# Reordering the TensorE products of the 63 steps that begin with a transform unit, in a fused spectral-mixing and hard-swish kernel

## The chip, the cores and the metric

The kernel runs on one core of one Trainium2 chip. The metric is the device time of one execution in microseconds; a kernel's time is the median of its runs. Beside it stands one profiled execution, whose trace gives the start and duration of each instruction on each engine: TensorE (PE, with its weight loads listed apart as PEld), VectorE (DVE), ScalarE (ACT), GpSimd (POOL) and SyncE (SP, which issues transfers here).

## What is computed

The reference is a global filter in the frequency domain, followed by a two-layer feed-forward block with hard-swish:

```python
X = np.fft.rfft(x, axis=1)                    # x: (8, 3008, 256)
Y = X * (filt_r + 1j * filt_i)[None]
y = np.fft.irfft(Y, n=3008, axis=1)
h = y.reshape(24064, 256) @ w_in              # w_in: (256, 2048)
g = h * np.clip(h + 3.0, 0.0, 6.0) / 6.0
out = g @ w_out                               # w_out: (2048, 256)
```

## The kernel before, in words

**Blocks and steps.** The 24064 tokens are cut into 47 blocks of 512, and the 2048 hidden columns into 8 parts of 256. One part of one block is a step, so there are 376 of them, in the order block by block and part by part. The first block (8 steps) is computed plainly. In the other 368 steps both matrix products are done as two-by-two block products with seven multiplications in place of eight. In step `i` the program issues the *up* products of its own part and, among them, the *down* (output) products of the part before, whose hidden values are then ready. The loop at the end of the function writes the order of a step out by hand, and each engine executes its own instructions in that order.

**The up products.** They are, in order of need, A11, S1, A12, S2, S4, S3 and A22 (in code `product(...)`, which ends in `strips` at L972). Each is 256 columns wide and is issued as two strips of 64 weight columns, four matmul records in all. They accumulate in two PSUM tiles with one buffer each: `al` takes A11, then S2, S3 and A22 on top of it; `be` takes S1 and S4 in one half and A12 in the other. Between them other engines read the partial sums:

- after A11, ACT copies `al` (L987, here called s0); after S1 and A12, ACT copies half of `be` (L988, s5); after S2, ACT copies `al` again (L997, s1);
- after S4, DVE adds `be` and the copies into the first hidden half (L1002, h0);
- after S3, DVE adds `al` and s5 into half of the second (L1007, h1);
- after A22, ACT copies `al` into the other half of the second (L1016, the h copy).

So S2 must wait for s0, S4 for s5, S3 for s1, A22 for h1, and whatever writes `al` next must wait for the h copy. The rectifier runs on ACT (L1021), once for each half, and the product with the hidden value on DVE (L1026).

**The output products.** DVE makes the seven operands from the hidden values: `g_sums` (L1026 for the second half, L1033, L1034) and `g_last` (L1039, which product 3 alone needs). The products are numbered 1 to 7. Each has two halves `u` of 128 columns; a half is four matmul records into a PSUM tile `po` that is read only at the end of a block. `down(k, p, *prods, us=...)` issues the numbered products in the order given.

**The transform units.** The transforms of the next batches are woven into these steps. `plan` says which function runs in which step and at which place of it. Three kinds of unit open a step (places 3 and 4 of the plan): the first stage (`a8_unit`, L608, 24 steps), the second stage (`b8_unit`, L706, 18 steps) and the inverse stage (`bi8_unit`, L779, 21 steps). Each consists of 32-row matmuls into four PSUM tiles, two of which are `al` and `be`. ACT copies these two out (L612, L712, L783), first `al`, then `be`. The step's own A11 and S1 write these tiles next, and so wait for the two copies.

In a step with a unit, `units` is a non-empty list, `inverse` is therefore true, and `ahead` is `(1, 2)`. No two such steps stand side by side; the step after one is always an ordinary step, which begins with A11. Product 3 of the step before can be held back behind the unit (`held`). Some steps also have an ACT copy for the next block's inputs (`t_copy`, L953) between the first rectifier and the h copy.

Of the kernel before, what the change touches and what calls it, by code (L numbers as in the profile page):

```python
# [53 lines left out]
NP = DFF // 256  # L54
# [175 lines left out]
def kernel(  # L230
# [602 lines left out]
    def pair(i):  # L833
        b, js, o, n = chunks[i]
        return b * HC * NA + o, n
# [134 lines left out]
    def strips(ps, w, x, **kw):  # L970
        for o in range(0, P, STRIP):
            nc.tensor.matmul(ps[ds(o, STRIP)], w[:, ds(o, STRIP)], x, skip_group_check=True, **kw)  # L972

    def product(ps, p, w, x, start=False, stop=False):
        strips(ps, w_in[p][:, w, :], x, start=start, stop=stop)
# [12 lines left out]
        nc.scalar.activation(out=s5, in_=be[:, 1, :], func=AXT.Copy)  # L988
        st["up"] = al, be, s, s5

    def up_2(k, p):
        t = st["xt", k]
        al, be, s, s5 = st["up"]
        h = [hp.tile([P, 512], FP32, name="h%d" % i) for i in range(2)]
        product(al, p, S2, t[:, F3, :])
        product(be[:, 1, :], p, S4, t[:, F5, :], stop=True)
        nc.scalar.activation(out=s[:, 1, :], in_=al, func=AXT.Copy)  # L997
        st["h"] = h
# [30 lines left out]
    def g_sums(k, p):  # L1029
        hswish(k, p, 1)  # L1030
        g = st["g", k, p]
        v = nc.vector
        v.tensor_tensor(out=g[:, G1, :], in0=g[:, G3, :], in1=g[:, G22, :], op=ALU.add)  # L1033
        v.tensor_tensor(out=g[:, G3:G2 + 1:2, :], in0=g[:, G3:G1 + 1, :],  # L1034
                        in1=g[:, G11:G11 + 1, :].broadcast_to([P, 2, 256]), op=ALU.subtract)

    def g_last(k, p):
        g = st["g", k, p]
        nc.vector.tensor_tensor(out=g[:, G4, :], in0=g[:, G12, :], in1=g[:, G2, :], op=ALU.subtract)  # L1039
# [7 lines left out]
    def down(k, p, *prods, us=(0, 1)):  # L1047
        g = st["g", k, p]
        if p == 0 and 1 in prods:
            st["po", k] = [psO.tile([P, 2, 2, P], FP32, name="po%d" % i) for i in range(4)]  # L1050
        for n in prods:
            bank, part = BANK[n]
            a, w = DOWN[n]
            for u in us:
                strips(st["po", k][bank][:, part, u, :], g[:, a, ts(u, P)], w_out[p][:, w, :],
                       start=(p == 0 and n in OPENS and u == 0), stop=(p == NP - 1 - (k == LAST)))

    def last_down():
        p, v, add = NP - 1, nc.vector.tensor_tensor, ALU.add
        g, o = st["g", LAST, p], st["o", LAST][0]  # L1060
        hswish(LAST, p, 1)
        ps = [psF.tile([P, 512], FP32, name="psf", tag="f") for t in range(2)]
        for i, a in ((0, G11), (1, G12)):
            for t in range(2):
                for u in range(2):
                    strips(ps[t][:, ts(u, D)], g[:, a + t, ts(u, P)], w_out[p][:, 2 * i:2 * i + 2, :].rearrange("p j m -> p (j m)"),
                           start=i == 0 and u == 0, stop=i == 1)
        out_4(LAST)
        v(out=o_at(LAST, 0, 1), in0=st["po", LAST][3][:, 1, :, :], in1=o_at(LAST, 0, 1), op=add)
        for t, qs in ((0, (nc.sync, nc.scalar)), (1, (nc.sync, nc.scalar))):  # L1070
            both = o[:, t, :, :].rearrange("p u d -> p (u d)")
            v(out=both, in0=ps[t], in1=both, op=add)
            store_last(t, qs)
# [6 lines left out]
    def plain_up(p):  # L1080
        st["g", 0, p] = gp.tile([P, 7, 256], FP32, name="g")
        st["h"] = [psU.tile([P, 512], FP32, name=n) for n in ("al", "be")]
        for i in range(2):
            for d in range(2):
                strips(st["h"][i], w_in[p][:, 2 * d + i, :], xn[:, d, :, 0:PAIRS], start=d == 0, stop=d == 1)
            relu(i)
            hswish(0, p, i)

    def plain_down(p, tokens=(0, 1)):
        g = st["g", 0, p]  # L1090
        if p == 0:
            st["po", 0] = [psO.tile([P, 2, 2, P], FP32, name="po%d" % i) for i in range(2)]
        for t in tokens:
            for u in range(2):
                for i, a in ((0, G11), (1, G12)):
                    strips(st["po", 0][t][:, u, :, :].rearrange("p a m -> p (a m)"), g[:, a + t, ts(u, P)],
                           w_out[p][:, 2 * i:2 * i + 2, :].rearrange("p j m -> p (j m)"),
                           start=p == 0 and u == 0 and i == 0, stop=p == NP - 1)
# [8 lines left out]
    def out_1(k):  # L1107
        po = st["po", k]
        p14 = p14p.tile([P, 2, 2, P], FP32, name="p14")
        nc.scalar.activation(out=p14, in_=po[0], func=AXT.Copy)  # L1110
        st["o", k] = op.tile([P, 2, 2, D], FP32, name="o", tag="o"), p14
# [76 lines left out]
    with tc.manual_schedule():  # L1188
# [120 lines left out]
        half = 0  # L1309
# [28 lines left out]
        for i in range(2, len(chunks)):  # L1338
            k = pair(i)[0] // PAIRS
# [57 lines left out]
        for n in range(1, B):  # L1397
            a_at, f_at, y_at, bi_at = places(n)
            if n > 1:
                k = (first[n] - 7) * NP  # L1400
# [4 lines left out]
            for c, s in enumerate(a_at):  # L1405
# [7 lines left out]
                k = (first[n] - 7) * NP  # L1413
# [44 lines left out]
        def late(i):  # L1458
            return i % NP in (1, 2) or any(fn in HEAVY for place in range(3) for fn, a in plan.get((i - 1, place), ()))

        held = None
        items = [(k, p) for k in range(NBLK) for p in range(NP)]
        for i in range(len(items) + 1):
            up = i < len(items)
            k, p = items[min(i, len(items) - 1)]
            dn = i > 0
            kd, pd = items[i - 1]
            def do(place):
                for fn, a in plan.get((i, place), ()):
                    fn(*a)  # L1470

            if k == 0:
                plain_up(p)
                do(0)
                if dn:
                    plain_down(pd)
                do(1)
                do(2)
                continue
            if not up:  # L1480
                last_down()
                break
            ends = k == LAST and p == NP - 1
            last_plain = dn and kd == 0
            dn = dn and kd > 0
            units = [fn for fn, a in plan.get((i, 3), ())]
            inverse = bool(units)
            ahead = (1, 2) if inverse else (1,) if units else ()
            if units:
                do(3)  # L1490
                if held:
                    down(*held, 3)
                g_sums(kd, pd)
                if not late(i):
                    g_last(kd, pd)
                do(4)
                down(kd, pd, *ahead)
                up_1(k, p)
                do(0)
                down(kd, pd, 4 if inverse else 2)  # L1500
            else:
                up_1(k, p)
                do(0)
                if dn:
                    g_sums(kd, pd)
                    if not late(i):
                        g_last(kd, pd)
                    down(kd, pd, 1)
            if up:
                up_2(k, p)  # L1510
            if dn and pd == 0 and kd > 1:
                out_4(kd - 1)
            if up:
                up_2b(k, p)
            if dn:
                down(kd, pd, *((5,) if inverse else (4,) if units else (2, 4)), us=(0,) if inverse else (0, 1))
                if pd == NP - 1:
                    out_1(kd)
            if up:
                up_3(k, p)  # L1520
                if dn and late(i) and not (pd == 0 and kd > 1):
                    g_last(kd, pd)
            if dn:
                down(kd, pd, 5, us=(1,) if inverse else (0, 1))
                down(kd, pd, 6)
            if up:
                up_4(k, p)
            if ends:
                out_1(k)
            if last_plain:  # L1530
                plain_down(pd, (0,))
            if dn and pd == 0 and kd > 1:
                out_5(kd - 1)
                g_last(kd, pd)
            if up:
                do(1)
                hswish(k, p, 0)
            if up:
                up_5(k, p)
            if last_plain:  # L1540
                plain_down(pd, (1,))
                plain_out()
            if dn:
                if pd == NP - 1 or ends:
                    out_2(kd)
                held = (kd, pd) if (i + 1, 3) in plan and any(fn is n_five for fn, a in plan.get((i, 0), ())) and kd not in kinds else None
                down(kd, pd, *((7,) if held else (7, 3)))
                if pd == NP - 1 or ends:
                    out_3(kd)
            do(2)  # L1550
# [30 lines left out]
```

## Time and profile before

| | |
|---|---|
| median of 3 runs | 2551.36 us (2550.79 to 2552.4) |
| the profiled execution | 2552.4 us, of which 2550.4 us is the span from first to last instruction |
| TensorE matmuls, busy | 2533.7 us (99%), 37890 records |
| TensorE weight loads, busy | 2000.0 us (78%) |
| VectorE, busy | 2016.9 us (79%) |
| ScalarE, busy | 1361.4 us (53%) |
| GpSimd, busy | 423.0 us (17%) |
| granted TensorE clock | 1.0 |
| transfers | 276.91 MB, mean 109 GB/s |

Busy time is the time in which at least one instruction of the engine was recorded as running. The ends of matmuls are modelled, so the 99% does not say that TensorE did useful work all the time; what it lost is seen in the distance from the start of one product to the start of the next. A record such as `MATMUL al<-xt,w_all ... x4` in the timeline is one whole up product; `po<-w_all,g x4`, `x8`, `x12` and `x16` are one to four halves of output products.

### The profile page before, as it was taken

What the parts mean: (1) busy time and instruction counts of PE and PEld (TensorE: products, weight loads), DVE (VectorE), ACT (ScalarE), POOL (GpSimd) and SP (SyncE); (2) the same over time, 40 slices, a digit from 0 to 9 for tenths busy, and PEclk for the clock granted to TensorE, in tenths of its full rate; (3) what the DMA queues carried; (4) which work ended last, traced back from release to release, by engine and by line L of the source; (5) the groups of instructions that cost most, each with busy time, mean ns of one, the idle gap of its engine ahead of it and who ended that gap; (6) DMA issues with size and microseconds to landing.
All of it is one profiled execution on the core that took longest, in us unless ns stands there. A gap on an engine that the chain in (4) does not pass through costs nothing.

```text
span 2550.4 us, 87284 instructions
## 1 busy us (share of the span) xinstructions
PE 2533.7 (99%) x37890; PEld 2000.0 (78%) x37890; DVE 2016.9 (79%) x3645; ACT 1361.4 (53%) x2836; POOL 423.0 (17%) x558
## 2 busy tenths in 40 slices
PE   8999999999999999999999999999999999999999
PEld 4478787777877778777887778877788777888887
DVE  6878888888787887877878788787887878766666
ACT  4554455555555555555555555555555555555554
POOL 3252111111211112111121111211102111011110
PEclk9999999999999999999999999999999999999999
DMA  8745556544445344444453443534434343211000
GB/s 232 235 124 165 161 137 153 161 133 100 117 97 137 97 103 118 97 129 98 112 119 87 131 107 99 134 89 116 118 70 96 88 102 88 52 45 26 19 22 26
DMA packets 210821, 276.91 MB, mean 109 GB/s; under 512 B 23274, under 2 KB 176392, under 8 KB 210054
## 3 DMA queue, kind: packets, MB, share of 16 engines
q1 hardware_dynamic: 163997, 200.76, 27.0%
q0 software_dynamic: 46112, 70.28, 14.2%
q8 instruction: 297, 4.87, 0.8%
q14 instruction: 86, 0.70, 0.1%
q10 hardware_dynamic: 329, 0.30, 0.0%
HBM read 164.38 MB, written 128.81 MB: 115 GB/s over the span
## 4 chain that ended last, share of the span: by engine, by line
PE 97%; DMA 2%; DVE 1%; SPq 0%; issue 0%; ACT 0%; POOL 0%; DVEq 0%
PE po L972 46%; PE al L972 26%; PE be L972 19%; PE psn L899 2%; PE be L608 1%; PE al L779 1%; PE psf L706 1%; DMA w_all<-in_x_dram 0%; PE psf L693 0%; DMA g_tmp<-t 0%; DMA ft<-in_filt_r_dram 0%; PE psf L589 0%; PE psn L972 0%; PE psf L763 0%; DMA w_all<-in_filt_r_dram 0%
## 5 line engine op out<-in xcount | busy, mean ns | idle before, releaser
L972 PEld LDWEIGHTS po<-w_all,g 128*64 128x64 f32 x20808 | 1235.9, 137 | 271.1 <-issue 35.4
L972 PE MATMUL po<-w_all,g 128*64 128x128 f32 (+1 forms) x20808 | 1417.6, 274 | 0.0
L1021 ACT ACTIVATE r<-h,half_c 128x512 f32<-128x512 f32 x736 | 531.1, 722 | 300.5 <-DVE h L1002 288.3
L972 PE MATMUL al<-xt,w_all 128*64 128x256 f32 x4416 | 668.1, 381 | 0.1
L1026 DVE SCALAR_TENSOR_TENSOR g<-r,h 128x512 f32<-128x512 f32 x736 | 518.4, 705 | 145.3 <-ACT r L1021 136.4
L972 PE MATMUL be<-xt,w_all 128*64 128x256 f32 x2944 | 442.6, 379 | 0.0
L1002 DVE TENSOR_TENSOR h<-be,s 128x512 f32<-128x512 f32 x368 | 254.0, 690 | 167.2 <-PE be L972 133.7
L972 PEld LDWEIGHTS be<-xt,w_all 128*64 128x64 f32 x2944 | 211.2, 137 | 106.5
L1016 ACT ACTIVATE h<-al 128x256 f32<-128x256 f32 x368 | 140.4, 382 | 272.1 <-PE al L972 269.8
L972 PEld LDWEIGHTS al<-xt,w_all 128*64 128x64 f32 x4416 | 273.1, 137 | 7.7 <-POOL w_all L469 1.0
L1007 DVE TENSOR_TENSOR h<-al,s 128x256 f32<-128x256 f32 x368 | 156.2, 425 | 149.1 <-PE al L972 148.9
L1034 DVE TENSOR_TENSOR g<-g 128x512 f32<-128x512 f32 x367 | 255.6, 697 | 12.6
L972 PE MATMUL al<-xn,w_all 128*64 128x256 f32 (+1 forms) x1536 | 239.8, 392 | 1.1 <-DVE g L1026 0.6
L972 PE MATMUL be<-xn,w_all 128*64 128x256 f32 (+1 forms) x1536 | 238.8, 391 | 0.0
L988 ACT ACTIVATE s<-be 128x256 f32<-128x256 f32 x368 | 141.0, 383 | 178.6 <-PE be L972 178.6
L997 ACT ACTIVATE s<-al 128x256 f32<-128x256 f32 x368 | 141.3, 384 | 151.5 <-PE al L972 151.3
L987 ACT ACTIVATE s<-al 128x256 f32<-128x256 f32 x368 | 141.5, 385 | 68.7 <-PE al L972 65.0
L1033 DVE TENSOR_TENSOR g<-g 128x256 f32<-128x256 f32 x367 | 161.8, 441 | 12.6
L972 PEld LDWEIGHTS be<-xn,w_all 128*64 128x64 f32 x1536 | 105.2, 137 | 69.8 <-issue 7.4
L1039 DVE TENSOR_TENSOR g<-g 128x256 f32<-128x256 f32 x367 | 155.9, 425 | 2.3
L958 POOL DMA_DIRECT2D xt<-xn x60 | 76.1, 1268 | 445.0 <-ACT xt L953 328.9
L1130 POOL TENSOR_TENSOR o<-p,o 128x256 f32<-128x256 f32 x45 | 33.0, 733 | 516.8 <-DVE o L1128 368.6
(199 smaller groups left out, 1971.9 us busy)
## 6 DMA issues: line engine op xcount, KB each, us to landing
g_tmp<-t POOLq DMA_DIRECT2D x96, 256.0 KB, 4.4
x_tmp<-in_x_dram SPq DMA_DIRECT2D x54, 384.0 KB
t<-g_tmp SPq DMA_DIRECT2D x168, 120.0 KB
ft<-f_tmp SPq DMA_DIRECT2D x36, 512.0 KB
t<-zp_tmp SPq DMA_DIRECT2D x36, 512.0 KB
o_tmp<-o SPq DMA_DIRECT2D x46, 256.0 KB
xt<-xn POOLq DMA_DIRECT2D x30, 384.0 KB, 6.4
zp_tmp<-y POOLq DMA_DIRECT2D x96, 96.0 KB, 3.7
```

The source lines that it names most:

```text
L972: nc.tensor.matmul(ps[ds(o, STRIP)], w[:, ds(o, STRIP)], x, skip_group_check=True, **kw)
L987: nc.scalar.activation(out=s[:, 0, :], in_=al, func=AXT.Copy)
L988: nc.scalar.activation(out=s5, in_=be[:, 1, :], func=AXT.Copy)
L997: nc.scalar.activation(out=s[:, 1, :], in_=al, func=AXT.Copy)
L1002: nc.vector.tensor_tensor(out=st["h"][0].rearrange("p (a n) -> p a n", a=2), in0=be, in1=s, op=ALU.add)
L1007: nc.vector.tensor_tensor(out=st["h"][1][:, 256:512], in0=al, in1=s5, op=ALU.add)
L1016: nc.scalar.activation(out=st["h"][1][:, 0:256], in_=al, func=AXT.Copy)
L1021: nc.scalar.activation(out=r, in_=st["h"][i], func=AXT.Relu, bias=half_c, scale=1.0 / 6.0)
L1026: nc.vector.scalar_tensor_tensor(out=st["g", k, p][:, o:o + 2, :].rearrange("p a n -> p (a n)"), in0=st["r", i], scalar=1.0, in1=st["h"][i ...
L1033: v.tensor_tensor(out=g[:, G1, :], in0=g[:, G3, :], in1=g[:, G22, :], op=ALU.add)
L1034: v.tensor_tensor(out=g[:, G3:G2 + 1:2, :], in0=g[:, G3:G1 + 1, :], in1=g[:, G11:G11 + 1, :].broadcast_to([P, 2, 256]), op=ALU.subtract)
L1039: nc.vector.tensor_tensor(out=g[:, G4, :], in0=g[:, G12, :], in1=g[:, G2, :], op=ALU.subtract)
```

## The change

In the steps that begin with a unit, the order of the products on TensorE changes. Nothing is added and nothing removed; the program before and the program after have the same instructions on ScalarE, VectorE, GpSimd and SyncE, in the same order. Ordinary steps are untouched.

```diff
-    def up_2(k, p):
+    def up_2(k, p, between=None):
 ...
         product(al, p, S2, t[:, F3, :])
+        if between:
+            between()
         product(be[:, 1, :], p, S4, t[:, F5, :], stop=True)
 ...
             units = [fn for fn, a in plan.get((i, 3), ())]
-            inverse = bool(units)
-            ahead = (1, 2) if inverse else (1,) if units else ()
 ...
-                down(kd, pd, *ahead)
+                down(kd, pd, 1, 2)
+                down(kd, pd, 4, us=(0,))
                 up_1(k, p)
                 do(0)
-                down(kd, pd, 4 if inverse else 2)
 ...
+            def half():
+                down(kd, pd, 4, us=(1,))
+                down(kd, pd, 5, us=(0,))
+
             if up:
-                up_2(k, p)
+                up_2(k, p, half if units else None)
 ...
-            if dn:
-                down(kd, pd, *((5,) if inverse else (4,) if units else (2, 4)), us=(0,) if inverse else (0, 1))
-                if pd == NP - 1:
-                    out_1(kd)
+            if dn and not units:
+                down(kd, pd, 2, 4)
+            if dn and pd == NP - 1:
+                out_1(kd)
 ...
-                down(kd, pd, 5, us=(1,) if inverse else (0, 1))
-                down(kd, pd, 6)
+                down(kd, pd, 5, us=(1,) if units else (0, 1))
+                down(kd, pd, *((6, 7) if units else (6,)))
 ...
-                down(kd, pd, *((7,) if held else (7, 3)))
+                down(kd, pd, *(() if units else (7,)), *(() if held else (3,)))
```

With 4a and 4b for the two halves of product 4, and so on, TensorE's order in such a step is:

| | |
|---|---|
| before | unit, 1, 2, A11, S1, A12, 4a, 4b, S2, S4, 5a, S3, 5b, 6, A22, 7, 3, then A11 of the next step |
| after | unit, 1, 2, 4a, A11, S1, A12, S2, 4b, 5a, S4, S3, 5b, 6, 7, A22, 3, then A11 of the next step |

## The prediction

> **What bounds the kernel now.** I read the chain of waits first. It ends in TensorE nearly everywhere, and in the lines of the up and output products:
>
> ```profile
> PE 97%; DMA 2%; DVE 1%; SPq 0%; issue 0%; ACT 0%; POOL 0%; DVEq 0%
> ```
>
> So time is lost or won only where TensorE stands still. I then read the timeline of TensorE in one of the 63 steps that change, a second-stage step, from the two output products behind the unit to A11 of the next step. Columns: start in us, length, line, tile:
>
> ```profile
> 1205.48 1.09 PE L972 MATMUL po<-w_all,g 128*64 128x128 f32 x16
> 1206.41 0.65 PE L972 MATMUL al<-xt,w_all 128*64 128x256 f32 x4
> 1206.89 0.65 PE L972 MATMUL be<-xn,w_all 128*64 128x256 f32 x4
> 1207.37 0.60 PE L972 MATMUL be<-xt,w_all 128*64 128x256 f32 x4
> 1207.80 0.61 PE L972 MATMUL po<-w_all,g 128*64 128x128 f32 x8
> 1208.24 0.60 PE L972 MATMUL al<-xt,w_all 128*64 128x256 f32 x4
> 1208.67 0.60 PE L972 MATMUL be<-xt,w_all 128*64 128x256 f32 x4
> 1209.10 0.39 PE L972 MATMUL po<-w_all,g 128*64 128x128 f32 x4
> 1209.32 0.65 PE L972 MATMUL al<-xt,w_all 128*64 128x256 f32 x4
> 1209.80 0.82 PE L972 MATMUL po<-w_all,g 128*64 128x128 f32 x12
> 1210.50 0.65 PE L972 MATMUL al<-xn,w_all 128*64 128x256 f32 x4
> 1210.98 1.04 PE L972 MATMUL po<-w_all,g 128*64 128x128 f32 x16
> 1211.86 0.39 PE L972 MATMUL al<-xt,w_all 128*64 128x256 f32 x2
> ```
>
> The reader should take differences of starts. Unhindered, an up product takes 0.43 (1207.37 to 1207.80), a whole output product 0.44, half of one 0.22. Where the product had to wait it takes 0.48: A11, S1, S3 and A22, four times 0.05. The twelve records before A22 take 0.70 instead of 0.65. These are the step's losses.
>
> What releases them is in the rows of ACT and DVE in the same step (s1, h0, h1, first rectifier, input copy, h copy):
>
> ```profile
> 1208.88 0.38 ACT L997 ACTIVATE s<-al 128x256 f32<-128x256 f32 x1 [0.48 <-PE al L972]
> 1209.39 0.69 DVE L1002 TENSOR_TENSOR h<-be,s 128x512 f32<-128x512 f32 x1 [1.48 <-PE be L972]
> 1210.02 0.42 DVE L1007 TENSOR_TENSOR h<-al,s 128x256 f32<-128x256 f32 x1
> 1210.11 0.73 ACT L1021 ACTIVATE r<-h,half_c 128x512 f32<-128x512 f32 x1 [0.85 <-DVE h L1002]
> 1210.74 0.61 ACT L953 ACTIVATE xt<-xn 128x512 f32<-128x512 f32 x1
> 1211.26 0.36 ACT L1016 ACTIVATE h<-al 128x256 f32<-128x256 f32 x1
> ```
>
> s1 ends at 1209.26 and S3 starts at 1209.32; h1 ends at 1210.44 and A22 starts at 1210.50. A release thus reaches TensorE 0.055 after the copy's end. For A22 the order is S4 at 1208.67, h0 0.72 later, h1 0.63 after h0's start, 0.42 long: 1.83 from S4 to A22. The waits of S1 for the unit's copy of `be` are in the list of waits (us in total, times, longest):
>
> ```profile
> PEld be L972 <- ACT t L612: 5.8, 23, 0.3
> PEld be L972 <- ACT t L783: 5.4, 21, 0.3
> PEld be L972 <- ACT t L712: 5.2, 18, 0.3
> ```
>
> Those 16.4 us are idle time of the weight loader, most of it covered by the matmuls before; by the starts, S1 loses 0.04 to 0.05 each time.
>
> Last, an undisturbed A22 and h copy, from the ordinary step just before:
>
> ```profile
> 1203.01 0.60 PE L972 MATMUL al<-xn,w_all 128*64 128x256 f32 x4
> ...
> 1203.65 0.38 ACT L1016 ACTIVATE h<-al 128x256 f32<-128x256 f32 x1 [1.09 <-PE al L972]
> ```
>
> The h copy starts 0.65 and ends 1.03 after A22's start, so `al` is free for the next writer at 1.03 + 0.055 = 1.087.
>
> **What the change removes.** I took the excess over 0.432, 0.436 and 0.218 (the same starts, read in ns) in all 63 steps: A11 and S1 lose 3.4 us in all, S3 3.3 us, A22 6.1 us: 12.8 us. In the new order, with T for A11's start, S1 follows at T+0.43, A12 at 0.86, S2 at 1.30, 4b 1.73, 5a 1.95, S4 2.16, S3 2.60, 5b 3.03, 6 3.25, 7 3.68, A22 4.12, product 3 4.55. Against that:
>
> - A11 and S1 come 0.22 later (4a is ahead of them). The copy of `be` holds S1 by 0.05, and that of `al` holds A11 by 0.05 to 0.07 where it does: both gone.
> - S2 needs s0, which is A11 + 0.65 + 0.38 + 0.055 = T+1.09. S2 loses the cover of product 4, but S1 and A12 keep it at T+1.30: no wait.
> - S4 needs s5, which starts 0.65 after A12: A12+1.09, and S4 comes at A12+1.30. No wait.
> - S3 needs s1: S2+1.08 to 1.09. It comes at S2+1.30 where it would have come at S2+1.08. The loss goes.
> - A22 needs h1: S4+1.83. It comes at S4 + 0.43 + 0.43 + 0.22 + 0.44 + 0.44 = S4+1.95, where without S3's loss it would have come at S4+1.74. The loss goes.
> - The moved output products: 4a needs what product 2 needs, ready at 1205.52 in the shown step; 5a is due at T+1.95, about 1208.6, and L1034 ends at 1206.71; product 7 needs the same instruction; product 3 needs L1039, done at S4+2.11, and comes at S4+2.39. No cost, and no DMA or queue of SP or POOL is passed by any of it.
>
> **What it adds.** Before, products 7 and 3 stood between A22 and the next step's A11: 0.43 + 0.87 = 1.30 from A22's unhindered start, against a release at 1.087. After, product 3 alone is left: 0.432 + 0.436 = 0.868. The next A11 waits 0.219 for the h copy. Nothing else is behind A22 in TensorE's queue to fill that, and the whole next step is queued behind A11. The trace of before has no wait at this place, so I bound it. From below it is 0.219. From above the weight load comes on top, as at all four losing products, whose 0.48 in place of 0.43 is that load laid open (A22 lost 0.04 before its weights and 0.05 with them): 0.268. I take 0.268, since the same kind of product shows it each time. A load that is late by less than its cover costs nothing: in the step at 946 us S1's load waits until 948.85 and S1 still starts 0.43 after A11. So S2, S3 and A22, whose releases come about when their load would start anyway, should pay nothing.
>
> The ACT queue decides when the h copy starts. The first rectifier, 0.72 after h0's start, and the input copy (in 30 of the 63 steps) stand ahead of it. In the shown step the h copy follows 0.52 behind the input copy's start, S4+2.59; A22 now ends its part at S4 + 1.95 + 0.65 = S4+2.60. Just free. One step (368.5 us) has two input copies and pays some 0.06 more there, and 0.04 at S3.
>
> The sum against the profiled execution: 2552.4 − 12.8 + 63 × 0.268 (16.9) + 0.1 = 2556.6, which is +4.2 us. With 0.219 it is +1.1. The median of the runs shown is 1.0 below the profiled execution, so the forecast is 2551.36 + 4.2 = 2555.6, 0.165% more.
>
> The Trainium skill bears on the 0.05: "TensorE: Matmul & The Clock Gate", Part 2, step-by-step, says that weight loads are pulled ahead of matmuls in flight. By that rule alone the load would lie in the shadow of product 3, and the sum would be +1.1. The trace speaks against it where the load itself carries the wait: 0.48 in place of 0.43.
>
> **The rivals.**
> - *Slower, by the loads of S2 and S3.* Their releases come 0.00 to 0.01 after the load would start (one matmul pair, 0.216, ahead). If such a late load is laid open in full once the product before it is in another chain, both pay 0.05: 63 × 0.10 = 6.3 on top, +10.5, 2561.9; one of them alone, 2558.7. It decides from a release later than the start less 0.05. Against it: the step at 946 us.
> - *Slower, by ACT.* If the input copy does not get out of the way in those 30 steps and the h copy starts 0.1 later, +3.0: 2558.6. For it: a margin of 0.01. Against it: the copies overlap in the shown rows.
> - *Faster, because the wait does not form.* If the next A11 is not tied to the h copy but only to h1, already past, only the 12.8 us remain: 2538.6. For it: no row of before shows TensorE waiting for L1016. Against it: `al` has one buffer and the h copy reads it.
> - *A shorter wait.* The load is hidden or the copy comes earlier: about +1, 2552.4.
>
> **How the numbers follow.** A measurement of this kernel tells about 0.2%, 5.1 us, from no change; the limit is 2556.5. The forecast has a chance of 0.62; it is 0.9 under the limit and three runs spread by 1.6, so 0.14 of it falls above. The rival of the loads has 0.10, that of ACT 0.14, the shorter wait 0.07, the faster case 0.07. Slower: 0.14 + 0.10 + 0.14 = 0.38. Within: 0.48 + 0.07 = 0.55. Faster: 0.07. The range goes from the shorter wait, 2552, to 2560, above ACT's case and one late load; it leaves out the faster case and the upper end of the loads.
>
> **What would show it.** In the changed kernel's timeline S1, S3 and A22 of these steps should take 0.43 and the records before A22 no more than their sum; A11 of the step after each should start 1.14 after A22, and the list of waits should have a new row of about 63 waits for L1016. I am wrong if that A11 starts 0.87 after A22, if S2 or S3 takes 0.48, or if the h copy starts later than 0.65 after A22.

## The result: 0.15% slower, and the profile after

| | median us | runs | range |
|---|---|---|---|
| before, same chip | 2550.39 | 22 | 2548.68 to 2553.97 |
| changed | 2554.22 | 22 | 2553.5 to 2556.3 |

The ratio is 1.0015, 95% interval 1.0009 to 1.0022: 3.8 us more. It is a real loss, though below the 0.2% that one measurement of three runs can tell.

The chain of waits of the changed kernel now has ACT in it, and its list by lines names the h copy (L1018 in the new numbering) with 1%:

```profile
PE 95%; ACT 2%; DVE 2%; DMA 1%; issue 0%; SPq 0%; DVEq 0%; POOL 0%
```

The same second-stage step as in the prediction, TensorE's timeline (start, length, line, tile), from the output products behind the unit to the first products of the next step:

```profile
1205.03 1.31 PE L972 MATMUL po<-w_all,g 128*64 128x128 f32 x20
1206.17 0.60 PE L972 MATMUL al<-xt,w_all 128*64 128x256 f32 x4
1206.60 0.60 PE L972 MATMUL be<-xn,w_all 128*64 128x256 f32 x4
1207.04 0.60 PE L972 MATMUL be<-xt,w_all 128*64 128x256 f32 x4
1207.47 0.60 PE L972 MATMUL al<-xt,w_all 128*64 128x256 f32 x4
1207.90 0.61 PE L972 MATMUL po<-w_all,g 128*64 128x128 f32 x8
1208.34 0.60 PE L972 MATMUL be<-xt,w_all 128*64 128x256 f32 x4
1208.77 0.60 PE L972 MATMUL al<-xt,w_all 128*64 128x256 f32 x4
1209.20 1.26 PE L972 MATMUL po<-w_all,g 128*64 128x128 f32 x20
1210.29 0.60 PE L972 MATMUL al<-xn,w_all 128*64 128x256 f32 x4
1210.72 0.61 PE L972 MATMUL po<-w_all,g 128*64 128x128 f32 x8
1211.37 0.65 PE L972 MATMUL al<-xt,w_all 128*64 128x256 f32 x4
1211.86 0.60 PE L972 MATMUL be<-xn,w_all 128*64 128x256 f32 x4
```

The h copy and the weight load of the next A11 in the same stretch, from the timeline of all engines (in brackets the loader's idle time and what ended it):

```profile
1210.94 0.38 ACT L1018 ACTIVATE h<-al 128x256 f32<-128x256 f32 x1
...
1211.37 0.20 PEld L972 LDWEIGHTS al<-xt,w_all 128*64 128x64 f32 x4 [0.29 <-ACT h L1018]
```

From A11 at 1206.17 down to product 3 at 1210.72 every product takes 0.43 or 0.44: no step loss is left at S1, S3 or A22. A22 starts at 1210.29, and product 3 is issued 0.43 later and lasts 0.44, to 1211.16. The h copy ends at 1211.32, and only then, at 1211.37, does the weight load of the next A11 start; S1 follows 0.49 behind it instead of 0.43. So 0.21 passes before the load, and 0.05 with it; over the 63 steps the median is 0.217 before the load, and 0.05 with it. The list of waits (us in total, times, longest) has the row that before did not have:

```profile
PEld al L972 <- ACT h L1018: 18.2, 63, 0.3
```

All 63 steps are in it, and the three rows in which S1's load waited for the unit's copies are gone.

The spans of the two profiled executions differ by 1.3 us only (2550.4 and 2551.7). The difference of 3.8 is in the part that was changed: the first unit starts at 204.4 us before and at 202.0 after (the start of the kernel, not touched, varies by that much from one execution to the next), and from there to the last unit it takes 1979.8 and 1983.5.

### The profile page after: what moved, and what is told of

Read it like the earlier page. It is cut to its first block, busy times and chain, and to the rows that moved or that the text cites. A ratio compares the mean times of both kernels' runs of the same rounds, so it can differ in the third digit from the quotient of the medians.

```text
span 2551.7 us, 87284 instructions
## 1 busy us (share of the span) xinstructions
PE 2534.1 (99%) x37890; PEld 2008.7 (79%) x37890; DVE 2013.2 (79%) x3645; ACT 1361.9 (53%) x2836; POOL 423.0 (17%) x558
## 4 chain that ended last, share of the span: by engine, by line
PE 95%; ACT 2%; DVE 2%; DMA 1%; issue 0%; SPq 0%; DVEq 0%; POOL 0%
PE po L972 44%; PE al L972 25%; PE be L972 19%; PE psn L899 2%; ACT h L1018 1%; PE be L608 1%; DVE h L1004 1%; PE al L779 1%; ACT xt L953 1%; PE psf L706 1%; PE psf L693 0%; DVE g L1041 0%; DVE h L1009 0%; DMA g_tmp<-t 0%; PE psf L589 0%
## 5 line engine op out<-in xcount | busy, mean ns | idle before, releaser
L972 PEld LDWEIGHTS al<-xt,w_all 128*64 128x64 f32 x4416 | 279.9, 137 | 38.0 <-ACT h L1018 18.2
L1018 ACT ACTIVATE h<-al 128x256 f32<-128x256 f32 x368 | 141.0, 383 | 274.6 <-PE al L972 273.4
L972 PEld LDWEIGHTS be<-xn,w_all 128*64 128x64 f32 x1536 | 110.5, 137 | 62.1 <-issue 7.4
```

Source lines behind the costliest of these rows:

```text
L1018: nc.scalar.activation(out=st["h"][1][:, 0:256], in_=al, func=AXT.Copy)
```

## The experiments

All were timed against the kernel before on one chip, where before was 2551.15 to 2551.17 us; the row of the changed kernel repeats the result above. Beside the time I give the loss in the trace: the time that TensorE's starts in the 63 steps, from the products behind the unit to the next A11, exceed 0.432, 0.436 and 0.218. The 0.05 behind every unit, alike in all kernels, is taken off; waits for output operands in a few steps, which the prediction's 12.8 left out, are in it.

| kernel | median us | ratio to before (95%) | loss in the 63 steps, us | loss less that of before |
|---|---|---|---|---|
| before | 2551.2 | 1 | 13.3 | |
| changed | 2554.22 (before 2550.39) | 1.0015 (1.0009 to 1.0022) | 17.1 | +3.8 |
| S1 first behind it | 2538.28 | 0.9950 (0.9937 to 0.9962) | 0.1 | −13.2 |
| 7 back | 2558.45 | 1.0027 (1.0015 to 1.0038) | 20.9 | +7.6 |
| half of 7 back | 2549.73 | 0.9994 (0.9984 to 1.0003) | 12.7 | −0.6 |
| before with S1 first | 2551.18 | 0.9999 (0.9990 to 1.0008) | 13.2 | −0.1 |
| none ahead | 2544.72 | 0.9972 (0.9962 to 0.9982) | 7.0 | −6.3 |
| S4 by S3 alone | 2547.86 | 0.9987 (0.9978 to 0.9996) | 10.9 | −2.4 |
| 4a ahead alone | 2548.48 | 0.9991 (0.9982 to 1.0000) | 10.8 | −2.5 |

In every row the last column agrees with the measured time to about 1 us.

**Take the new wait away: S1 first behind a unit step.** The theory is that the loss is the next A11 waiting for the h copy. A11 writes `al`; S1 writes `be`, which has long been free. So S1 can stand in the gap:

```diff
-    def up_1(k, p):
+    def up_1(k, p, behind=False):
 ...
+        if behind:
+            product(be[:, 1, :], p, S1, xb(k, 0, 1), start=True)
         product(al, p, A11, t[:, F1, :], start=True)
-        product(be[:, 1, :], p, S1, xb(k, 0, 1), start=True)
+        if not behind:
+            product(be[:, 1, :], p, S1, xb(k, 0, 1), start=True)
 ...
             else:
-                up_1(k, p)
+                up_1(k, p, (i - 1, 3) in plan)
```

> The changed kernel, but in the 63 steps that follow a unit step S1 (into be) is issued ahead of A11 (into al). Theory (the changed kernel loses 0.267 us at A11 behind each unit step, because al is freed by the h copy 1.087 us after A22 and only product 3 stands between; S1 adds 0.432 of cover): A11 comes at A22+1.30 and waits for nothing; 63 x 0.267 = 16.8 us come back, 2554.2 - 16.8 = 2537.4, ratio to before 0.995. Rival 1 (the next step is held by the ScalarE queue as a whole, the second rectifier above all, not by the h copy alone): S1 or A11 still waits, at most half comes back, ratio 0.998 or more. Rival 2 (nothing was won and nothing lost, the two kernels only differ by noise): ratio 1.000 to 1.002.

It took 2538.28 us, ratio 0.9950. The timeline of the step (here the h copy is L1021; `...` stands for rows left out):

```profile
1203.26 0.60 PE L972 MATMUL al<-xn,w_all 128*64 128x256 f32 x4
...
1203.69 0.61 PE L972 MATMUL po<-w_all,g 128*64 128x128 f32 x8
1203.91 0.38 ACT L1021 ACTIVATE h<-al 128x256 f32<-128x256 f32 x1
...
1204.13 0.60 PE L972 MATMUL be<-xn,w_all 128*64 128x256 f32 x4
...
1204.56 0.60 PE L972 MATMUL al<-xt,w_all 128*64 128x256 f32 x4
1204.99 0.60 PE L972 MATMUL be<-xt,w_all 128*64 128x256 f32 x4
```

S1 starts at 1204.13, before the h copy ends at 1204.29, and A11 at 1204.56, 1.30 behind A22. Nothing waits: the whole 0.267 is back, and with it the gain of the change, which the new wait had eaten, is laid open. Both rivals fall: with the ScalarE queue unchanged nothing waits, and the gain is far outside the noise. This kernel beats the two others.

**The control: S1 first in the kernel before.** The same edit of `up_1`, without the change.

> The kernel before, with S1 ahead of A11 in the steps behind a unit step, as a control. Theory: before, products 7 and 3 already cover the h copy (1.30 against 1.087), so S1 first is worth nothing: ratio 1.000, within 1 us. Rival (S1 first is good in itself, whatever stands before it): faster by some of the 16.8 us.

It took 2551.18 us against 2551.15. S1 first is worth nothing where products 7 and 3 already cover the h copy; its worth in the run above comes from the change.

**Undo one part: 7 back behind A22.**

```diff
-                down(kd, pd, *((6, 7) if units else (6,)))
+                down(kd, pd, 6)
 ...
-                down(kd, pd, *(() if units else (7,)), *(() if held else (3,)))
+                down(kd, pd, *((7,) if held else (7, 3)))
```

> The changed kernel with product 7 put back behind A22 in the unit steps; the rest of the change stays. Theory: A11 behind the step waits no more (-0.267), but A22 comes at S4 + 0.43 + 0.43 + 0.22 + 0.44 = S4+1.52 and is released at S4+1.83, so it waits 0.316 and its load 0.05 is laid open, 0.365. 63 x (0.365 - 0.267) = +6.2 us over the changed kernel: 2560.4, ratio to before 1.004. Rival (A22 does not need the cover, the move of product 7 was the only harm): the 16.8 us come back, 2537.4, ratio 0.995.

It took 2558.45 us, 7.3 above before where 10 were expected; the direction and the place are right. Columns as above, from S4 on:

```profile
1212.74 0.60 PE L972 MATMUL be<-xt,w_all 128*64 128x256 f32 x4
...
1214.54 0.65 PE L972 MATMUL al<-xn,w_all 128*64 128x256 f32 x4
```

A22 is released 1.80 after S4, not 1.83, so a step loses 0.33 (0.277 of wait and 0.05 of weight load) instead of 0.365. Before, h1 had also waited for S3, which came late by its own 0.05, and started 0.63 after h0; with S3 directly behind S4 it starts 0.61 after h0, and takes 0.41 instead of 0.42. A part of A22's loss before was thus handed on from S3.

**Half of it: only the second half of 7 back.** Product 7 is split by `us=(0,)` ahead of A22 and `us=(1,)` behind it.

> The changed kernel with the second half of product 7 alone put back behind A22 in the unit steps, three halves behind A22 instead of two. Theory: A11 of the next step comes at A22 + 0.432 + 0.654 = 1.086 against a release at 1.087, so only its load is laid open, 0.05. A22 comes at S4 + 0.43 + 0.43 + 0.22 + 0.44 + 0.22 = S4+1.74; the run with all of 7 put back showed its release at S4+1.80, so it waits 0.06 and its load 0.05, 0.11. In all 0.16 a step, 63 x 0.16 = 10.1 us against 12.8 before and 16.8 changed: ratio to before 0.999, 6.7 us under the changed kernel. Rival (the wait behind A22 does not go down half by half, TensorE stands until some fixed point): as the changed kernel, ratio 1.0015.

It took 2549.73 us, ratio 0.9994. The time alone does not tell it from before, but its interval leaves out the changed kernel's 1.0015, so the wait does go down with each half and the rival falls. The loss in the trace is 12.7 us, not the 10.1 expected. A22 lost 0.11 as foreseen, and behind the steps without an input copy A11 lost its load of 0.05. Behind the 30 with one it lost 0.13:

```profile
1209.89 0.65 PE L972 MATMUL al<-xn,w_all 128*64 128x256 f32 x4
...
1210.16 0.61 ACT L953 ACTIVATE xt<-xn 128x512 f32<-128x512 f32 x1
...
1210.37 0.83 PE L972 MATMUL po<-w_all,g 128*64 128x128 f32 x12
1210.68 0.36 ACT L1018 ACTIVATE h<-al 128x256 f32<-128x256 f32 x1
...
1211.10 0.65 PE L972 MATMUL al<-xt,w_all 128*64 128x256 f32 x4
```

A22 comes earlier than in the changed kernel, the rectifier and the input copy on ACT do not, so the h copy starts 0.79 behind A22's recorded start. In the steps of this run without an input copy it is 0.70: the 0.65 from before and the 0.05 of A22's own late load. The rest is the ACT rival of the prediction; since the h copy is here also 0.02 shorter, it costs A11 0.08. In the changed kernel the rival does not act, by a margin of 0.01.

**Another split: none of product 4 ahead.** 1 and 2 ahead of A11; 4 between S2 and S4; 5, 6 and 7a ahead of A22; 7b and 3 behind.

> Another split of the same 14 halves in the unit steps: products 1 and 2 alone ahead of A11 as before, 4 whole between S2 and S4, then S4, S3, 5, 6 and the first half of 7 ahead of A22, and the second half of 7 and 3 behind it. Theory: S1 and A11 lose the 3.4 us of before again; S3 and A22 lose nothing (S4 to A22 is 1.95 as in the changed kernel); A11 of the next step comes at A22 + 0.432 + 0.654 = 1.086 against 1.087, so only its load is laid open, 63 x 0.05 = 3.2 us. In all 6.6 us of losses against 12.8 before and 16.9 changed: 2550.4 - 6.2 = 2544.2, ratio 0.9976. Rival (a load that is late costs nothing unless the matmul itself is late): 2541, ratio 0.9963.

It took 2544.72 us against 2544.2 expected. A11 of the next step lost its load (0.05) and no more, though that A11 was recorded only 0.001 late: a load that starts when its matmul is due is laid open in full. The rival, by which such a load is free (2541), falls.

**The parts alone.** S2 ahead of 4 and S4 next to S3, with nothing else moved, is the changed kernel without 4a ahead of `up_1`, with `down(kd, pd, 4)` as `half`, `down(kd, pd, 5, 6)` ahead of A22 and `7, 3` behind it; 4a ahead alone adds one `down(kd, pd, 4, us=(0,))` ahead of `up_1` to the kernel before and leaves 4b where 4 was.

> One part of the change alone: S2 ahead of product 4 and S4 next to S3; 4a is not moved ahead of A11, and 5, 6 and 7 stay where they were (unit, 1, 2, A11, S1, A12, S2, 4, S4, S3, 5, 6, A22, 7, 3). Theory: A11 and S1 lose the 3.4 us of before; S3 comes at S2+1.30 against 1.08 and loses nothing (-3.3); A22 comes at S4+1.74 against 1.80 and loses 0.11, 6.9 us in place of 6.1; A11 of the next step has products 7 and 3 ahead of it and loses nothing. In all 10.3 us against 12.8: ratio 0.999, 2.5 us faster than before. Rival (this order is the whole gain of 12.8): ratio 0.995 or near it.

> One part of the change alone, in the kernel before: the first half of product 4 ahead of A11, nothing else moved (unit, 1, 2, 4a, A11, S1, A12, 4b, S2, S4, 5a, S3, 5b, 6, A22, 7, 3). Theory: A11 and S1 lose nothing (-3.4 us), but S4 now comes at A12 + 0.43 + 0.22 + 0.43 = 1.08 against 1.087, so its load of 0.05 is laid open (+3.2 to 3.6); S3 and A22 lose what they lost before. The gain is given back in the same step: ratio 1.000, within 1 us. Rival (the copies of the unit's tiles were the wait that counted): 3.4 us faster, ratio 0.9987.

The first took 2547.86, 3.3 us faster, as expected within the interval: S3's loss went and A22 lost 0.11. The second took 2548.48, 2.7 us faster with an interval that reaches the expected 1.000 and also holds the rival's 0.9987, so the time alone does not decide. The trace shows what happened: S4's load was laid open (0.05, 3.2 us in all) as expected, which the rival left out, but S3, now 0.05 later itself, lost nothing, for its load still had 0.05 left. A22 then waited longer and lost 1.0 us more in all. Each part alone wins something, together with 7 moved they remove everything (0.1 us in the first run), and moving 7 makes the wait that is larger than all of it.

## Why the prediction was right

- *What the change removes.* Forecast: nothing lost at A11, S1, S3 and A22, 12.8 us. Shown by the timeline of after, and by the run with S1 first, which is 12.9 us faster than before. One reading was loose: S1 lost 0.04 to 0.05 in 52 of the 63 steps, not each time; the 3.4 us in all stand.
- *What it adds.* Forecast: 0.219 of wait and 0.05 of weight load, 0.268 at each of 63 A11, 16.9 us in all. The trace has 0.217 (0.278 in the one step with two input copies) and 0.05 at each of the 63; the changed kernel (+3.8) and the one with S1 first (−12.9) lie 16.7 us apart, each against its own before. The upper bound was the right one to take. The sign given for it, A11 at 1.14 after A22, did not come: A11 is recorded at 1.085, since the recorded start of a product that waits comes with its load (both rows above are at 1211.37). The 0.05 is seen behind it, in the 0.48 to S1, as the prediction itself had read it at the four losing products.
- *The sum.* +4.2 forecast, +3.8 measured; 2555.6 against 2554.22, the before of that comparison being 1.0 lower than the median known then.
- *The late loads of S2 and S3.* Forecast as free, and the trace shows 0.00 extra at all 63. S2's load comes only 0.003 after its slot, S3's in one step alone is clearly late, with 0.07 still left to its matmul. The slower rival falls.
- *The step with two input copies.* Of its 0.1, the 0.06 at A11 came; the 0.04 at S3 did not.
- *The weight load.* By the rule of the Trainium skill ("TensorE: Matmul & The Clock Gate", Part 2, step-by-step) that loads are pulled ahead of matmuls in flight, the 0.05 would have been hidden. In these traces loads do start up to 0.216 ahead of their matmul, but one that is released only when its matmul is due cannot: 0.05 at each of the 63.
- *ACT.* Forecast as just free, by 0.01: right for the changed kernel, and the half-way run shows the rival's mechanism where A22 comes earlier.
- *The faster rival* (A11 not tied to the h copy): refuted by the new row of waits.
- *One size was off.* A22's release was put at S4+1.83; with S3 moved up it is S4+1.80. In the changed kernel nothing depends on it, since A22 comes at 1.95; it made the expectation with 7 back 2.3 us too high.

## What to carry to other kernels

Where an accumulator has one buffer, each read of its partial sum by another engine needs some fixed amount of other work behind it on the engine that writes (for the products of this kernel 1.09 us from A11, A12, S2 or A22, and 1.80 from S4 over two DVE sums to A22); count the filler at every such place before moving any, because work that covers one wait was covering another. The last wait of a step is paid in the next one, so look there. When the filler runs out, look for a product that writes another accumulator and can change places, which cost nothing here (2551.18 against 2551.15).

## What the runs showed of the hardware

- A late weight load costs what it lacks of 0.05 us. When it comes as the matmul is due it is laid open in full, whatever the wait before (0.05 with a wait of 0.001, of 0.217 and of 0.277). With 0.01 left it costs 0.04 (S1 in the kernel before, 34 steps), and with 0.05 left nothing (S3 in the run with 4a ahead alone, 63 steps).
- The new wait repeats to about 0.002 us from step to step, apart from the one step with two input copies. Single executions of one kernel spread by up to 6.5 us (2548.12 to 2554.64). Part of such a spread lies ahead of the changed steps: the nine profiled executions, whose kernels are the same up to there, reach the first unit between 201.2 and 204.5 us.
